# Attention operands spread anew over GpSimd, VectorE and ScalarE, and a pair's weighted sums in one stretch

## The chip, the cores and the metric

The kernel runs on one core of one Trainium2 chip. The metric is device time in microseconds for one execution, the median of several runs. The kernel before takes 841.28 us (three runs, 840.67 to 841.33). The engines that matter are TensorE (PE: matrix products and transposes into PSUM), VectorE (DVE), ScalarE (ACT), GpSimd (POOL) and the queue of SyncE (SP), which issues most transfers.

## The reference

Attention over 4 batches, 8 heads, 576 positions and 64 columns per head, with a causal mask in blocks of 64; then a mixture of eight experts (one per token) and a last two-layer network. The change touches the attention alone:

```python
scores = scale * np.matmul(q, k.transpose(0, 1, 3, 2))
scores = np.where(mask, scores, -1000000000.0)
scores = scores - np.max(scores, axis=-1, keepdims=True)
attn = np.exp(scores)
attn = attn / (np.sum(attn, axis=-1, keepdims=True) + 1e-09)
return np.matmul(attn, v).astype(np.float32)
```

## The kernel before, in words

Attention goes over 16 pairs of heads (`n` = 0 to 15). A pair has seven steps (`z` = 0 to 6), one block of scores each: 64-position blocks are taken two by two, for one head or for both. In most pairs the order of the blocks is `ORDER` = 3, 1, 0, 4, 2, 6, 5. Block 6 (`kinds` 4, all 576 columns, both heads) comes at step 5.

In each step TensorE makes the scores of the step (`scores`, tile `s`) and then transposes the exponentials of the block two steps earlier (`flip`, tile `pt`). VectorE takes the row maxima (`nmax`, lines 339, 344, 348), ScalarE the exponentials (line 350, tile `pall`), and one of them copies `pt` into `pT` (line 379 on ScalarE, line 511 on VectorE).

A score is a product in three terms: each of `q` and `k` is split into a high part of reduced precision and the low part that is left. `qa` holds the high and low parts of q, `qb` copies of the high parts, `kd` k's high parts twice (in both halves of the partitions), `kl` k's low parts, `qf` and `kT` the plain values for block 0. `load_q` and `load_k` make these for the pair after the one whose scores are running.

What stands between the steps is in a table, `PLAN`: the key is (step, place), where place 0 is ahead of the step's scores, 1 behind the scores, and 2 behind the step's softmax. "q" and "k" transpose the next pair's operands into PSUM (`psq`, `psk`) and split them. A tuple such as (0, 3) makes the weighted sums of the pair before over those blocks of keys (`weigh`, tile `px`, line 393, in halves of TensorE's columns). "first" makes the sums of the first 64 positions (`py`, line 408), and, where the pair is the second of two, puts the row factors in place on VectorE (`row_order`, lines 429 and 435). "store" copies `px` to `xT` and, where the pair is the second of two, puts four or five rows on a list. "rows" takes one of that list (tile `xr`, line 445, then two VectorE operations, lines 451 and 455, and a store).

PSUM has eight banks. Two hold `s`, two `pt` and `py`, two `px` and `xr` (tag "x"), and the last two are one buffer of tag "big". That one buffer is taken in turn by `psq`, `psk` and the scores of block 6: the next owner's first matmul waits until every reader of the owner before is done.

Each engine works its instructions off in the order of the program. Behind the attention, the routing and the experts follow; the first steps of the routing are laid between the steps of pairs 14 and 15. Rows that are still on the list when attention ends are made at the start of the experts (`begin`).

Of the kernel before, what the change touches and what calls it, by code (L numbers as in the profile page):

```python
# [11 lines left out]
F32 = mybir.dt.float32  # L12
# [6 lines left out]
ALU = mybir.AluOpType  # L19
# [6 lines left out]
P = 128  # L26
B, H, S, D = 4, 8, 576, 64
# [5 lines left out]
E, F = 8, 1024  # L33
# [16 lines left out]


ORDER_FIRST, ORDER_LAST, ORDER = (2, 4, 0, 1, 5, 6, 3), (3, 1, 4, 2, 6, 0, 5), (3, 1, 0, 4, 2, 6, 5)
PLAN = {(1, 0): ["rows", "q"], (2, 0): ["sum"], (2, 2): ["k", (0, 3)], (3, 0): ["rows"],
        (4, 2): [(3, 5)], (5, 0): ["first"], (5, 1): ["store"], (6, 2): ["rows"]}
FROM = 0, 128, 256, 320, 448
LAG = 2
COPY = 4
ON_ACT = (0, 2, 3, 4, 5)


KDUP = (1, 1, 0, 0), (0, 0, 1, 1)
SMALL = (1, 1, 1, 1, 1, 1, 1, 2), (2, 2, 2, 2, 1, 1, 2, 2)
EARLY = 3, 2
WARM = 30, 2
BIG = 3e38
# [57 lines left out]
def attention(late, weights, tc, q, k, v, ids, w_gate, mbias, x_dram, dram, ident, tabs):  # L123
# [3 lines left out]
    nc = tc.nc  # L127
# [6 lines left out]
    wk = ctx.enter_context(tc.tile_pool(name="a_wk", bufs=2))  # L134
# [47 lines left out]
    def turned(dst, x):  # L182
        if x.dtype == F32R:
            nc.tensor.transpose(dst.bitcast(F32R), x, identr)
        else:
            nc.tensor.transpose(dst, x, ident)
# [20 lines left out]
    qzs = [one.tile([P, P], F32R, name=f"qz{i}") for i in range(2)]  # L207
# [34 lines left out]

    qk = {}

    def eng(n, x):
        return nc.gpsimd if SMALL[n > 0][x] == 2 else nc.vector

    def load_q(n):
        psq = ps2.tile([P, 1024], F32, tag="big", name=f"psq{n}")
        psq = psq[:, 64:64 + S]  # L250
        for t, x in enumerate(FROM):
            turned(psq[:, x:x + P], io_t[n, "q"][:, t, :])
        qa, qb, qf = qas[n % 2], qbs[n % 2], qfs[n % 2]

        qT = wk.tile([P, 9, 64], F32, tag="qT", name=f"qT{n}", bufs=1)
        nc.scalar.activation(qT, psq.rearrange("p (i t) -> p i t", t=64), AF.Copy, scale=D ** -0.5)
        for h in range(2):
            hs, oh = slice(h * 64, h * 64 + 64), slice(64 - h * 64, 128 - h * 64)
            nc.scalar.copy(qa[hs, h, :7], qT[hs, 2:])
            eng(n, h).tensor_tensor(qa[oh, h, :7], qT[hs, 2:], qa[hs, h, :7].bitcast(F32), op=ALU.subtract)  # L260
        for h in range(2):
            hs = slice(h * 64, h * 64 + 64)
            (nc.gpsimd.tensor_copy if n else nc.scalar.copy)(
                qf[hs, h].rearrange("p (i t) -> p i t", t=64), qT[hs, :2])
        eng(n, 4).tensor_copy(qb[:64, :7], qa[:64, 0, :7])
        eng(n, 5).tensor_copy(qb[64:, 7], qa[64:, 1, 6])
        eng(n, 6).tensor_copy(qb[64:, 8:], qa[64:, 1, :6])
        eng(n, 7).tensor_copy(qzs[n % 2][:, 64:], qa[:, 1, 6])

    def load_k(n):  # L270
        if n:
            psk = ps2.tile([P, 1024], F32, tag="big", name=f"psk{n}")[:, 64:64 + S]
            ranges = [(psk, slice(0, S))]
        else:

            pk = [ps2.tile([P, 512], F32, tag="x", name=f"psk{n}_{i}", bufs=2) for i in range(2)]
            ranges = [(pk[0][:, :448], slice(0, 448)), (pk[1][:, :P], slice(448, S))]
        for t, x in enumerate(FROM):
            if n:
                dst = psk[:, x:x + P]  # L280
            else:
                dst = pk[t // 4][:, x % 448:x % 448 + P]
            turned(dst, io_t[n, "k"][:, t, :])
        kT = wk.tile([P, S], F32, tag="kT", name=f"kT{n}")
        for a, cs in ranges:
            nc.vector.tensor_copy(kT[:, cs], a)
        kd = wk.tile([P, 2, S], F32R, tag="kd", name=f"kd{n}")
        kl = wk.tile([P, S], F32R, tag="kl", name=f"kl{n}")
        for h in range(2):
            hs, oh = slice(h * 64, h * 64 + 64), slice(64 - h * 64, 128 - h * 64)  # L290
            for u, dst in enumerate((kd[hs, h], kd[oh, h])):
                e = KDUP[n > 0][2 * h + u]
                if e == 0:
                    for a, cs in ranges:
                        nc.scalar.copy(dst[:, cs], a[hs])
                else:
                    (nc.vector if e == 1 else nc.gpsimd).tensor_copy(dst, kT[hs])
            eng(n, 2 + h).tensor_tensor(kl[hs], kT[hs], kd[hs, h].bitcast(F32), op=ALU.subtract)
        qk[n] = kT, kd, kl

    pTs, nmaxs = {}, {}
# [84 lines left out]
    def weigh(n, k0, k1):  # L386

        if k0 == 0:
            pxs[n] = ps2.tile([P, 512], F32, tag="x", name=f"px{n}", bufs=2)
        for kk in range(k0, k1):  # L390
            s0 = max(64, kk * P)
            for h in range(2):
                nc.tensor.matmul(pxs[n][h * 64:(h + 1) * 64, s0 - 64:], io_t[n, "v"][:, kk, h * D:(h + 1) * D],  # L393
                                 pTs[n][:, kk, h, s0:], start=(kk == 0), stop=(kk == 4))

    def store_xT(n):
        b, c = divmod(n, NP)
        nc.scalar.copy(xT[:, c, b % 2 * S + 64:(b % 2 + 1) * S], pxs.pop(n))

    def weigh_first(n, order=True):  # L400

        b, c = divmod(n, NP)
        if n < B * NP - 1:
            px = ps1.tile([P, 512], F32, tag="pt", name=f"py{n}", bufs=4 - SB)
        else:
            px = ps2.tile([P, 512], F32, tag="x", name=f"py{n}", bufs=2)
        for h in range(2):
            nc.tensor.matmul(px[h * 64:(h + 1) * 64, :64], io_t[n, "v"][:, 0, h * D:(h + 1) * D],
                             pTs[n][:, 0, h, :64], start=True, stop=True)
        if c % 2 and order:  # L410
            row_order(b, c // 2)
        nc.scalar.copy(xT[:, c, b % 2 * S:b % 2 * S + 64], px[:, :64])

    def row_sums(b, a):

        r = rinv[:, b, 2 * a:2 * a + 2]
        nc.vector.tensor_scalar(r, ssum[:, b, 2 * a:2 * a + 2], 1e-9, None, op0=ALU.add)
        nc.vector.reciprocal(r, r)
# [18 lines left out]
    def rows(j, a, spare=False, xr=None):  # L437

        if spare:
            px = ps2.tile([P, 1024], F32, tag="big", name=f"xr{j}_{a}")  # L440
        else:
            px = ps2.tile([P, 512], F32, tag="x", name=f"xr{j}_{a}", bufs=2)
        w = P + 2 * E
        for c in range(2):
            nc.tensor.matmul(px[:, c * w:(c + 1) * w], xT[:, 2 * a + c, j % NB * P:(j % NB + 1) * P],
                             rh[:, 2 * a + c, :], start=True, stop=True)
        if xr is None:
            xr = keep.tile([P, 256], F32, tag="xr", name=f"xrow{j}_{a}", bufs=4)
        pv = px[:, :2 * w].rearrange("p (c w) -> p c w", w=w)
        rv = rt[:, j, 4 * a:4 * a + 4].rearrange("p (c h) -> p c h", h=2)  # L450
        nc.vector.tensor_tensor(
            xr.rearrange("p (c h d) -> p c h d", c=2, h=2),
            pv[:, :, :P].rearrange("p c (h d) -> p c h d", h=2),
            rv.unsqueeze(3).to_broadcast([P, 2, 2, D]), op=ALU.mult)
        nc.vector.tensor_tensor(
            lg[:, j, 4 * a:4 * a + 4, :].rearrange("p (c h) e -> p c h e", h=2),
            pv[:, :, P:].rearrange("p c (h e) -> p c h e", h=2),
            rv.unsqueeze(3).to_broadcast([P, 2, 2, E]), op=ALU.mult)
        nc.sync.dma_start(out=x_dram[j * P:(j + 1) * P, a * 256:(a + 1) * 256], in_=xr)
# [9 lines left out]
    def act(n, z, at):  # L469

        if n >= B * NP:
            return
        for what in PLAN.get((z, at), ()):
            if what == "q" and n + 1 < B * NP:
                load_q(n + 1)
            elif what == "k" and n + 1 < B * NP:
                load_k(n + 1)
            elif what == "rows" and todo:
                done.add(todo[0])
                rows(*todo.pop(0))  # L480
            elif n == 0:
                continue
            elif isinstance(what, tuple):
                weigh(n - 1, *what)
            elif what == "sum" and (n - 1) % 2:
                row_sums((n - 1) // NP, (n - 1) % NP // 2)
            elif what == "first":
                weigh_first(n - 1)
            elif what == "store":
                store_xT(n - 1)  # L490
                if (n - 1) % 2:
                    todo.extend((j, (n - 1) % NP // 2) for j in rows_of[(n - 1) // NP])
# [5 lines left out]
    for g in range(len(steps) + LAG):  # L498
        n, z = divmod(g, NK)
# [1081 lines left out]
```

## Time and profile before

| | |
|---|---|
| median of three runs | 841.28 us |
| the profiled execution | 839.69 us |
| its span | 837.8 us |
| PE busy | 817.9 us (98%) |
| DVE busy | 608.3 us (73%) |
| ACT busy | 495.6 us (59%) |
| POOL busy | 205.4 us (25%) |

The attention is the first 224 us or so of the span. The rows below name instructions by the lines of the kernel before. In a timeline neighbouring instructions of one group stand in one row, whose duration runs from the first one's start to the last one's end. Matmuls overlap, so the step from one row's start to the next is the better measure of what TensorE spends.

### The profile page before, as it was taken

What the parts mean: (1) busy time and instruction counts of PE and PEld (TensorE: products, weight loads), DVE (VectorE), ACT (ScalarE), POOL (GpSimd) and SP (SyncE); (2) the same over time, 40 slices, a digit from 0 to 9 for tenths busy, and PEclk for the clock granted to TensorE, in tenths of its full rate; (3) what the DMA queues carried; (4) which work ended last, traced back from release to release, by engine and by line L of the source; (5) the groups of instructions that cost most, each with busy time, mean ns of one, the idle gap of its engine ahead of it and who ended that gap; (6) DMA issues with size and microseconds to landing.
All of it is one profiled execution on the core that took longest, in us unless ns stands there. A gap on an engine that the chain in (4) does not pass through costs nothing. (4 is left out here: it accounts for less than half of the span.)

```text
span 837.8 us, 13997 instructions
## 1 busy us (share of the span) xinstructions
PE 817.9 (98%) x4936; PEld 709.3 (85%) x4936; DVE 608.3 (73%) x1115; ACT 495.6 (59%) x994; POOL 205.4 (25%) x249
## 2 busy tenths in 40 slices
PE   6999999998899999999999999999999999999998
PEld 5777777775788888888888999999999988888887
DVE  6788888789666656797873766766636877777774
ACT  5898888896533334464544666766657644444442
POOL 8546556546301212120202000110000011112120
PEclk6999999999999999999999999999999999999999
DMA  6445655630744447765625453453644633333301
GB/s 155 119 125 144 172 145 134 171 95 20 247 131 150 153 125 234 240 204 163 203 84 162 142 176 121 170 175 134 218 120 160 239 143 128 125 126 126 132 32 38
DMA packets 138058, 123.17 MB, mean 147 GB/s; under 512 B 70183, under 2 KB 122423, under 8 KB 135296
## 3 DMA queue, kind: packets, MB, share of 16 engines
q1 hardware_dynamic: 132256, 107.98, 41.9%
q0 software_dynamic: 4384, 13.92, 4.7%
q8 instruction: 40, 0.66, 0.3%
q10 hardware_dynamic: 1344, 0.33, 0.2%
q14 instruction: 34, 0.28, 0.1%
HBM read 89.17 MB, written 40.37 MB: 155 GB/s over the span
## 5 line engine op out<-in xcount | busy, mean ns | idle before, releaser
L1019 PE MATMUL h<-yhi,wi 128*128 128x384 f32 x768 | 200.4, 338 | 1.1 <-ACTq L1253 1.1
L1019 PEld LDWEIGHTS h<-yhi,wi 128*128 128x128 f32 x768 | 139.5, 188 | 1.5 <-ACTq L1253 1.5
L1019 PE MATMUL h<-ylo,wi 128*128 128x384 f32 x384 | 129.2, 337 | 0.0
L1293 ACT ACTIVATE cl<-h,half 128x384 f32<-128x384 f32 x96 | 55.9, 582 | 69.4 <-PE h L1019 69.1
L350 ACT ACTIVATE pall<-s,nmax 128x384 f32<-128x384 f32 (+2 forms) x144 | 79.5, 558 | 28.1 <-DVE nmax L344 17.0
L1297 DVE SCALAR_TENSOR_TENSOR gg<-cl,h 128x384 f32<-128x384 f32 x96 | 52.3, 552 | 51.8 <-ACT cl L1294 49.7
L1423 PE MATMUL p<-wo,s 128*128 128x256 f32 (+1 forms) x432 | 87.8, 338 | 0.0
L1423 PEld LDWEIGHTS p<-wo,s 128*128 128x128 f32 x432 | 68.5, 188 | 9.2
L1478 POOL DMA_INDIRECT out_dram<-rest,tab x16 | 27.3, 1707 | 190.9 <-DVE rest L1445 185.4
L1019 PEld LDWEIGHTS h<-ylo,wi 128*128 128x128 f32 x384 | 72.1, 188 | 0.0
L368 PE MATMUL pt<-ident,pall 128*128 128x128 f32 x400 | 65.7, 282 | 5.5 <-DVE pT L511 3.5
L1423 PE MATMUL p<-wo,a 128*128 128x256 f32 (+1 forms) x330 | 66.0, 335 | 0.0
L1019 PE MATMUL h<-xhi,wh 128*128 128x512 f32 (+2 forms) x164 | 63.1, 385 | 0.0
L1019 PE MATMUL h<-xhi,wl 128*128 128x512 f32 (+2 forms) x164 | 61.7, 376 | 0.5 <-DVE wl L1103 0.5
L1019 PE MATMUL h<-xlo,wh 128*128 128x512 f32 (+2 forms) x164 | 61.6, 376 | 0.0
L1128 PE MATMUL acc<-wh,hl 128*128 128x512 f32 x152 | 59.6, 392 | 0.1
L1423 PEld LDWEIGHTS p<-wo,a 128*128 128x128 f32 x330 | 52.8, 188 | 7.9
L1128 PE MATMUL acc<-wl,hh 128*128 128x512 f32 x152 | 59.3, 390 | 0.0
L1128 PE MATMUL acc<-wh,hh 128*128 128x512 f32 x152 | 59.1, 389 | 0.0
L393 PE MATMUL px<-pT,v 128*64 128x448 f32 (+4 forms) x320 | 54.5, 432 | 0.0
L1294 ACT ACTIVATE cl<-cl 128x384 f32<-128x384 f32 x96 | 50.5, 526 | 3.0
L368 PEld LDWEIGHTS pt<-ident,pall 128*128 128x128 f32 x400 | 43.9, 143 | 7.0 <-issue 3.1
(316 smaller groups left out, 1807.8 us busy)
## 6 DMA issues: line engine op xcount, KB each, us to landing
raw<-in_moe_w_dram SPq DMA_DIRECT2D x80, 256.0 KB
g_dram<-gg SPq DMA_DIRECT2D x48, 384.0 KB
g<-g_dram SPq DMA_DIRECT2D x18, 1024.0 KB
wi_raw<-in_moe_w_in_dram SPq DMA_DIRECT2D x16, 512.0 KB
wo_raw<-in_moe_w_out_dram SPq DMA_DIRECT2D x16, 512.0 KB
yr<-y_dram SPq DMA_DIRECT2D x18, 256.0 KB
x_dram<-xrow SPq DMA_DIRECT2D x33, 128.0 KB
v<-in_v_dram SPq DMA_DIRECT2D x32, 128.0 KB
```

What stands on the lines that cost most here:

```text
L350: nc.scalar.activation(pall[n % 2][:, o:o + w], pss[:, u:u + w], AF.Exp, bias=nm[:, x:x + 1], scale=1.0, accum_out=ssum[:, b, c, x:x + 1])
L368: nc.tensor.transpose(pt[:, kk, :], pa[:, o + kk * P:o + (kk + 1) * P], ident)
L393: nc.tensor.matmul(pxs[n][h * 64:(h + 1) * 64, s0 - 64:], io_t[n, "v"][:, kk, h * D:(h + 1) * D], pTs[n][:, kk, h, s0:], start=(kk == 0), ...
L1019: nc.tensor.matmul(ps, a[za], b[zb], start=(i == 0), stop=(i == n - 1))
L1128: nc.tensor.matmul(accs[s][u], a[:, us], b[:, 1, :], start=(f == 0 and i == 0), stop=(f == NF - 1 and i == 2))
L1293: nc.scalar.activation(cl, ph, AF.Relu, bias=half, scale=0.5)
L1294: nc.scalar.activation(cl, cl, AF.Square)
L1297: nc.vector.scalar_tensor_tensor(gg[:, :, f % 2, :], cl.rearrange(t3, t=P), 1.0, ph.rearrange(t3, t=P), op0=ALU.min, op1=ALU.max)
L1423: nc.tensor.matmul(o, a, b, start=(x == 0 and i in FRESH), stop=(x == len(terms) - 1), skip_group_check=True)
L1478: outs.append(nc.gpsimd.indirect_dma_start(out=out[:, :], out_offset=bass.IndirectOffsetOnAxis(ap=tabs.tab[:, j, 0:1].bitcast(U32), axis=0 ...
```

## The change

Four things change. The high parts of q go from ScalarE to GpSimd, for every pair but the first, with all that `load_q` copies besides. k's high parts are wanted twice per head; ScalarE made both of the first head from PSUM and VectorE both of the second from `kT`. Now ScalarE makes one per head from PSUM, and GpSimd makes the other from it. The low parts of k are subtracted on VectorE straight from PSUM, at a place "low" of their own in the table; only 128 columns of plain k are still copied. And the weighted sums of all five blocks with "first" stand in one stretch behind step 2, with "store" in step 3 and the rows at step 4 where step 3 had them.

```diff
--- before.py
+++ after.py
@@ -50,16 +50,15 @@
 ORDER_FIRST, ORDER_LAST, ORDER = (2, 4, 0, 1, 5, 6, 3), (3, 1, 4, 2, 6, 0, 5), (3, 1, 0, 4, 2, 6, 5)
-PLAN = {(1, 0): ["rows", "q"], (2, 0): ["sum"], (2, 2): ["k", (0, 3)], (3, 0): ["rows"],
-        (4, 2): [(3, 5)], (5, 0): ["first"], (5, 1): ["store"], (6, 2): ["rows"]}
+PLAN = {(1, 0): ["rows", "q"], (2, 0): ["sum"], (2, 2): ["k", (0, 5), "first"], (3, 1): ["store"],
+        (3, 2): ["low"], (4, 0): ["rows"], (6, 2): ["rows"]}
 FROM = 0, 128, 256, 320, 448
 LAG = 2
 COPY = 4
 ON_ACT = (0, 2, 3, 4, 5)
-KDUP = (1, 1, 0, 0), (0, 0, 1, 1)
-SMALL = (1, 1, 1, 1, 1, 1, 1, 2), (2, 2, 2, 2, 1, 1, 2, 2)
+KDUP = 1, 1, 0, 0
 EARLY = 3, 2
 WARM = 30, 2
 BIG = 3e38
@@ -242,9 +241,6 @@
     qk = {}
-    def eng(n, x):
-        return nc.gpsimd if SMALL[n > 0][x] == 2 else nc.vector
-
     def load_q(n):
         psq = ps2.tile([P, 1024], F32, tag="big", name=f"psq{n}")
         psq = psq[:, 64:64 + S]
@@ -254,18 +250,24 @@
         qT = wk.tile([P, 9, 64], F32, tag="qT", name=f"qT{n}", bufs=1)
         nc.scalar.activation(qT, psq.rearrange("p (i t) -> p i t", t=64), AF.Copy, scale=D ** -0.5)
-        for h in range(2):
-            hs, oh = slice(h * 64, h * 64 + 64), slice(64 - h * 64, 128 - h * 64)
-            nc.scalar.copy(qa[hs, h, :7], qT[hs, 2:])
-            eng(n, h).tensor_tensor(qa[oh, h, :7], qT[hs, 2:], qa[hs, h, :7].bitcast(F32), op=ALU.subtract)
-        for h in range(2):
-            hs = slice(h * 64, h * 64 + 64)
-            (nc.gpsimd.tensor_copy if n else nc.scalar.copy)(
-                qf[hs, h].rearrange("p (i t) -> p i t", t=64), qT[hs, :2])
-        eng(n, 4).tensor_copy(qb[:64, :7], qa[:64, 0, :7])
-        eng(n, 5).tensor_copy(qb[64:, 7], qa[64:, 1, 6])
-        eng(n, 6).tensor_copy(qb[64:, 8:], qa[64:, 1, :6])
-        eng(n, 7).tensor_copy(qzs[n % 2][:, 64:], qa[:, 1, 6])
+        E = nc.gpsimd if n else nc.vector
+        copy = nc.gpsimd.tensor_copy if n else nc.scalar.copy
+        halves = [(h, slice(h * 64, h * 64 + 64), slice(64 - h * 64, 128 - h * 64)) for h in range(2)]
+        for h, hs, oh in halves:
+            copy(qa[hs, h, :7], qT[hs, 2:])
+            if not n:
+                E.tensor_tensor(qa[oh, h, :7], qT[hs, 2:], qa[hs, h, :7].bitcast(F32), op=ALU.subtract)
+        if n:
+            for h, hs, oh in halves:
+                E.tensor_tensor(qa[oh, h, :7], qT[hs, 2:], qa[hs, h, :7].bitcast(F32), op=ALU.subtract)
+        for h, hs, oh in halves:
+            copy(qf[hs, h].rearrange("p (i t) -> p i t", t=64), qT[hs, :2])
+        E.tensor_copy(qb[:64, :7], qa[:64, 0, :7])
+        E.tensor_copy(qb[64:, 7], qa[64:, 1, 6])
+        E.tensor_copy(qb[64:, 8:], qa[64:, 1, :6])
+        nc.gpsimd.tensor_copy(qzs[n % 2][:, 64:], qa[:, 1, 6])
+
+    low_k = {}
     def load_k(n):
         if n:
@@ -281,21 +283,28 @@
             else:
                 dst = pk[t // 4][:, x % 448:x % 448 + P]
             turned(dst, io_t[n, "k"][:, t, :])
-        kT = wk.tile([P, S], F32, tag="kT", name=f"kT{n}")
-        for a, cs in ranges:
-            nc.vector.tensor_copy(kT[:, cs], a)
+        kT = wk.tile([P, S if n == 0 else P], F32, tag="kT" if n else "kT0", name=f"kT{n}", bufs=2 if n else 1)
         kd = wk.tile([P, 2, S], F32R, tag="kd", name=f"kd{n}")
         kl = wk.tile([P, S], F32R, tag="kl", name=f"kl{n}")
-        for h in range(2):
-            hs, oh = slice(h * 64, h * 64 + 64), slice(64 - h * 64, 128 - h * 64)
-            for u, dst in enumerate((kd[hs, h], kd[oh, h])):
-                e = KDUP[n > 0][2 * h + u]
-                if e == 0:
-                    for a, cs in ranges:
-                        nc.scalar.copy(dst[:, cs], a[hs])
-                else:
-                    (nc.vector if e == 1 else nc.gpsimd).tensor_copy(dst, kT[hs])
-            eng(n, 2 + h).tensor_tensor(kl[hs], kT[hs], kd[hs, h].bitcast(F32), op=ALU.subtract)
+        halves = [(h, slice(h * 64, h * 64 + 64), slice(64 - h * 64, 128 - h * 64)) for h in range(2)]
+        if n:
+            nc.vector.tensor_copy(kT, psk[:, :P])
+            for h, hs, oh in halves:
+                nc.scalar.copy(kd[hs, h], psk[hs])
+            for h, hs, oh in halves:
+                nc.gpsimd.tensor_copy(kd[oh, h], kd[hs, h])
+            low_k[n] = [(kl[hs], psk[hs], kd[hs, h].bitcast(F32)) for h, hs, oh in halves]
+        else:
+            for a, cs in ranges:
+                nc.vector.tensor_copy(kT[:, cs], a)
+            for h, hs, oh in halves:
+                for u, dst in enumerate((kd[hs, h], kd[oh, h])):
+                    if KDUP[2 * h + u] == 0:
+                        for a, cs in ranges:
+                            nc.scalar.copy(dst[:, cs], a[hs])
+                    else:
+                        nc.vector.tensor_copy(dst, kT[hs])
+                nc.vector.tensor_tensor(kl[hs], kT[hs], kd[hs, h].bitcast(F32), op=ALU.subtract)
         qk[n] = kT, kd, kl
     pTs, nmaxs = {}, {}
@@ -475,6 +484,9 @@
                 load_q(n + 1)
             elif what == "k" and n + 1 < B * NP:
                 load_k(n + 1)
+            elif what == "low" and n + 1 in low_k:
+                for dst, a, b in low_k.pop(n + 1):
+                    nc.vector.tensor_tensor(dst, a, b, op=ALU.subtract)
             elif what == "rows" and todo:
                 done.add(todo[0])
                 rows(*todo.pop(0))
```

TensorE, steps 2 to 5 of pair 7 before (`px6`, `py6` are pair 6's weighted sums, `s7_6` block 6 of pair 7):

```order
L393 MATMUL px6_1578<-pT6_1374,v6_918 64x320 x2
L445 MATMUL xr6_0_1589<-rh_161,xT_162 128x144 x2
L326 MATMUL s7_4_1596<-kd7_1391,qa1_137 128x512
...
L326 MATMUL s7_2_1608<-kd7_1391,qa1_137 128x384
...
L368 MATMUL pt7_0_0_1612<-ident_65,pall1_158 128x128 x2
L393 MATMUL px6_1578<-pT6_1374,v6_918 64x192 x2
L393 MATMUL px6_1578<-pT6_1374,v6_918 64x64 x2
L408 MATMUL py6_1622<-pT6_1374,v6_918 64x64 x2
L316 MATMUL s7_6_1626<-kd7_1391,qa1_137 128x288
```

The same stretch in the changed kernel:

```order
L402 MATMUL px6_1583<-pT6_1374,v6_918 64x320 x2
L402 MATMUL px6_1583<-pT6_1374,v6_918 64x192 x2
L402 MATMUL px6_1583<-pT6_1374,v6_918 64x64 x2
L417 MATMUL py6_1594<-pT6_1374,v6_918 64x64 x2
L335 MATMUL s7_4_1602<-kd7_1390,qa1_137 128x512
...
L454 MATMUL xr7_0_1617<-rh_161,xT_162 128x144 x2
L335 MATMUL s7_2_1624<-kd7_1390,qa1_137 128x384
...
L377 MATMUL pt7_0_0_1628<-ident_65,pall1_158 128x128 x2
L325 MATMUL s7_6_1634<-kd7_1390,qa1_137 128x288
```

The sums of the last two blocks and `py` stood between the transposes of step 4 and block 6; they now stand ahead of step 3. One row (`xr`) stands between step 3 and block 6, before in step 3's front and now behind its transposes.

VectorE from step 1 to step 5 of pair 7 before (`qb0`, `kT8`, `kd8` belong to pair 8):

```order
L265 COPY qb0_138<-qa0_136 64x448
L266 COPY qb0_138<-qa0_136 64x64
L344 TENSOR_REDUCE nmax7_1488<-s7_1_1534 128x2
L344 TENSOR_REDUCE nmax7_1488<-s7_0_1549 128x2
L286 COPY kT8_1568<-psk8_1562 128x576
L297 CAST kd8_1570<-kT8_1568 64x576 x2
...
L348 TENSOR_REDUCE nmax7_1488<-s7_4_1596 128x1
L511 COPY pT7_1553<-pt7_1_0_1600 128x2x2x128
L348 TENSOR_REDUCE nmax7_1488<-s7_2_1608 128x1
L339 TENSOR_REDUCE nmax7_1488<-s7_6_1626 128x1
```

And in the changed kernel:

```order
L353 TENSOR_REDUCE nmax7_1495<-s7_1_1541 128x2
L353 TENSOR_REDUCE nmax7_1495<-s7_0_1556 128x2
L291 COPY kT8_1575<-psk8_1569 128x128
L357 TENSOR_REDUCE nmax7_1495<-s7_4_1602 128x1
L523 COPY pT7_1560<-pt7_1_0_1607 128x2x2x128
L489 TENSOR_TENSOR kl8_1577<-psk8_1569,kd8_1576 64x576 x2
...
L357 TENSOR_REDUCE nmax7_1495<-s7_2_1624 128x1
L348 TENSOR_REDUCE nmax7_1495<-s7_6_1634 128x1
```

The casts of `qb`, most of `kT` and the doubles `kd` are gone; two subtractions that read `psk8` stand behind the copy of step 3.

GpSimd's work for pair 8 before (`qa0`, `qb0`, `qz0` and `kl8` belong to it):

```order
L263 COPY qf0_140<-qT8_1522 64x128 x2
L260 TENSOR_TENSOR qa0_136<-qT8_1522,qa0_136 64x448 x2
L267 COPY qb0_138<-qa0_136 64x384
L268 COPY qz0_142<-qa0_136 128x64
L298 TENSOR_TENSOR kl8_1571<-kT8_1568,kd8_1570 64x576 x2
```

And in the changed kernel:

```order
L257 CAST qa0_136<-qT8_1529 64x448 x2
L262 TENSOR_TENSOR qa0_136<-qT8_1529,qa0_136 64x448 x2
L264 COPY qf0_140<-qT8_1529 64x128 x2
L265 COPY qb0_138<-qa0_136 64x448
L266 COPY qb0_138<-qa0_136 64x64
L267 COPY qb0_138<-qa0_136 64x384
L268 COPY qz0_142<-qa0_136 128x64
L295 COPY kd8_1576<-kd8_1576 64x576 x2
```

The two subtractions for `kl` went; the casts of `qa`, two copies into `qb` and two copies of `kd` came.

## Rows read from the trace of the kernel before

**Rows 1.** Windows: length, busy us (instructions) per engine, PE clock, DMA share, GB/s.

```profile
12.15:24.69 12.54, 11.81 (x62) 9.72 (x62) 8.13 (x14) 9.35 (x26) 7.59 (x10) 0.63 0.72 176
36.34:186.46 150.12, 149.25 (x1152) 113.52 (x1150) 123.26 (x265) 130.90 (x361) 83.66 (x100) 1.00 0.55 143
```

**Rows 2.** TensorE's timeline, one pair: start, duration, operation, count, idle before.

```profile
101.78 2.76 PE L393 MATMUL px<-pT,v 128*64 128x512 f32 x12
104.47 0.76 PE L445 MATMUL xr<-rh,xT 128*128 128x144 f32 x4
104.97 0.49 PE L326 MATMUL s<-kd,qa 128*128 128x512 f32 x1
105.53 0.20 PE L329 MATMUL s<-maskk,maskq 128*128 128x64 bf16 x1
...
106.78 0.66 PE L393 MATMUL px<-pT,v 128*64 128x192 f32 x8
107.49 0.40 PE L316 MATMUL s<-kd,qa 128*128 128x288 f32 x1
...
109.69 0.66 PE L445 MATMUL xr<-rh,xT 128*128 128x144 f32 x4
110.09 0.43 PE L326 MATMUL s<-kd,qa 128*128 128x384 f32 x1
```

**Rows 3.** VectorE's timeline beside it.

```profile
101.55 0.85 DVE L266 CAST qb<-qa 64x64 fp32r<-64x64 f32 x1 [0.20 <-ACT qa L259]
102.42 1.02 DVE L344 TENSOR_REDUCE nmax<-s 128x2 f32<-128x512 f32 x2
...
105.77 0.69 DVE L348 TENSOR_REDUCE nmax<-s 128x1 f32<-128x512 f32 x1
106.38 0.68 DVE L511 COPY pT<-pt 128x512 f32<-128x512 f32 x1
106.98 0.55 DVE L348 TENSOR_REDUCE nmax<-s 128x1 f32<-128x384 f32 x1
```

**Rows 4.** ScalarE's timeline there.

```profile
100.36 1.15 ACT L259 CAST qa<-qT 64x448 fp32r<-64x448 f32 x2
101.54 0.59 ACT L379 COPY pT<-pt 128x512 f32<-128x512 f32 x1
```

**Rows 5.** Groups of instructions by line: busy us, mean ns, idle before.

```profile
L298 DVE TENSOR_TENSOR kl<-kT,kd 64x576 fp32r<-64x576 f32 x2 | 1.5, 754 | 0.1
L77 DVE TENSOR_TENSOR xlo<-xt,xhi 128x512 fp32r<-128x512 f32 x8 | 5.4, 690 | 8.2 <-ACT xhi L76 8.0 <-issue 0.2
...
L298 POOL TENSOR_TENSOR kl<-kT,kd 64x576 fp32r<-64x576 f32 x30 | 45.2, 1505 | 11.6 <-DVE kd L297 9.8
L267 POOL CAST qb<-qa 64x384 fp32r<-64x384 f32 x15 | 7.6, 506 | 0.9
```

**Rows 6.** TensorE's timeline in the last pair.

```profile
205.67 2.37 PE L393 MATMUL px<-pT,v 128*64 128x512 f32 x12
207.97 0.51 PE L445 MATMUL xr<-rh,xT 128*128 128x144 f32 x2
```

**Rows 7.** TensorE's timeline in an even pair.

```profile
63.87 2.95 PE L393 MATMUL px<-pT,v 128*64 128x512 f32 x12
66.75 0.50 PE L326 MATMUL s<-kd,qa 128*128 128x512 f32 x1
...
68.57 0.66 PE L393 MATMUL px<-pT,v 128*64 128x192 f32 x8
69.59 0.40 PE L316 MATMUL s<-kd,qa 128*128 128x288 f32 x1
```

**Rows 8.** VectorE's timeline under the routing of the first slots.

```profile
190.27 1.12 DVE L265 CAST qb<-qa 64x448 fp32r<-64x448 f32 x1
...
194.95 0.94 DVE L297 CAST kd<-kT 64x576 fp32r<-64x576 f32 x2
```

**Rows 9.** VectorE's timeline in the even pair of group 7.

```profile
69.77 1.12 DVE L429 COPY rt<-rinv 128x16 f32<-128x16 f32 x1
```

## The prediction

> **What bounds the kernel now.** I read the engines' shares by stretch first. In the twelve pairs from 36.34 to 186.46 us TensorE is busy 149.25 of 150.12 us at the full granted clock (1.00, the 2.4 GHz level), ScalarE 130.90, VectorE 123.26, GpSimd 83.66 [rows 1]. A pair takes 150.12 / 12 = 12.51 us, and TensorE hardly ever has nothing in flight. So whatever moves the attention must move TensorE: by shortening what it runs, or by making it wait. Since matmuls overlap, I then took TensorE's timeline of one pair and read the steps from start to start, not the durations [rows 2]. The other engines' timelines beside it [rows 3, 4] tell what each was doing while TensorE was in the weighted sums.
>
> Two things are to be seen there. VectorE stands behind ScalarE's casts of q: the cast of 64 columns runs from 101.55 for 0.85 us, and the maxima of step 1 begin only at 102.42 [rows 3]. ScalarE spends 1.15 us on those casts ahead of the copy of `pT` at 101.54 for which the weighted sums wait [rows 4]. And between the start of step 3's mask product (105.53) and block 6 (107.49) TensorE has 1.96 us of work [rows 2]; that is the cover under which the one "big" buffer of PSUM has to come free, since block 6 takes it from `psk`.
>
> **The change, part by part.**
>
> *The low parts of k on VectorE, from PSUM.* This is the part that decides. Before, the last readers of `psk` were ScalarE's copies and the copy of `kT`. Now the two subtractions read it too, and they stand on VectorE behind step 3's maxima and behind its copy into `pT`. How late that is can be read off: the mask product starts at 105.53, the maxima at 105.77, the copy at 106.38, VectorE is free at 106.98, thus 1.45 us behind the mask [rows 2, 3]. Nothing of this chain can come earlier, since each link needs step 3's scores or transposes. For one subtraction of 64x576 with one operand in PSUM there is no row. Below it lies the 128x512 one with an operand in PSUM, 690 ns, above it the same shape out of SBUF on VectorE in the first pair, 754 ns [rows 5]; as shape and count of columns agree I take 754. Two are 1.51 us, so the buffer is free 1.45 + 1.51 = 2.96 us behind the mask, and with 0.04 us of handing over (the maxima start 0.04 us after the mask's end, 105.73) block 6 starts 3.00 us behind it.
>
> When would TensorE be there? Of the 1.96 us, 0.71 (106.78 to 107.49) were the second stretch of weighted sums, which is gone from this place: 1.25 is left. A row of `xr` comes in, 0.40 us (109.69 to 110.09) [rows 2]. Less 0.05 to 0.1 for entering the sums that no longer follow, it is there after about 1.6 us. It waits 3.00 - 1.60 = 1.40 us, in every pair, with all of its later work behind it; VectorE's maxima of step 4 are then late too, but their exponentials are wanted only two steps on, and by the durations above they arrive about when TensorE does. With 690 ns the wait is 1.27; were the subtraction to cost 0.9, it is 1.7.
>
> *The weighted sums in one stretch.* The first stretch takes 2.69 us from its start to the next row's in pair 7 [rows 2], but 2.30 in the last pair, where nothing was waited for [rows 6]. In an even pair, where step 3 follows directly, it takes 2.88, and the second stretch takes 1.02 (68.57 to 69.59) against the 0.71 of pair 7 [rows 7]. A row of `xr` behind the sums takes 0.50 (104.47 to 104.97) and elsewhere 0.40, so leaving the stretch costs about 0.1, and I take the same for entering. So, odd pairs gain 0.39 of waits and 0.2 for one entry and exit less, 0.59; even pairs 2.88 - 2.40 = 0.48 (2.30 and 0.1 for leaving, which the row behind it carries there), 0.31 of the second stretch and 0.2, 0.99. Mean 0.79. The waits go because ScalarE no longer has its 1.15 us of casts there and VectorE no longer stands behind them.
>
> In the Trainium skill, "TensorEngine Tiling (Array Packing)", section Key Properties, a change of tiling mode drains TensorE. The 0.50 against 0.40 agrees with that in kind; the page has no price. Without such a drain the gain would be 0.2 less per pair.
>
> *q and the doubles of k on GpSimd.* GpSimd loses two subtractions of 1505 ns and gains two casts of 448 columns, two small copies and two copies of 576. A one-operand cast of 384 columns takes 506 ns [rows 5]; by columns 0.6 and 0.75 us. So 3.0 us go and about 1.2 + 0.8 + 1.5 = 3.5 come, on an engine busy 83.66 of 150.12. At worst (each copy at the 1505 of two operands) it is 3 us more, and the doubles are wanted only at step 0 of the next pair, over 4 us after block 6's old place. I cost it at nothing.
>
> *What VectorE and ScalarE are rid of* costs nothing where TensorE sets the pace. It counts in pair 14, where the routing's first steps fill VectorE: there `qb` (1.12 and some 0.4), the doubles (0.94) [rows 8] and 0.45 of `kT` go, 1.5 comes and one row's 0.6 of VectorE moves in: about -0.8 us. The rows' list is one step earlier in each pair, so one of six rows left over for the experts' start is already made: -0.4 us.
>
> *Sum.* Per pair +1.40 - 0.79 = +0.61 us, for the 13 pairs 1 to 13: +7.9. Pair 0 has no weighted sums and runs at a mean clock of 0.63 [rows 1], so TensorE is slower to arrive and waits little: +0.3. With -0.8 and -0.4 this is +7.0 us. On the profiled execution's 839.69 (its span 837.8 and 1.9 around it) that is 846.7; the median of the runs shown is 1.6 higher, 841.28, and from there it is 848.3. I say 848.3, for the pairs' terms with their bounds 844 to 854.
>
> **The rivals.**
>
> *More hidden waits in TensorE's steps.* A busy TensorE is modelled, and 0.39 us of waits were found within one group that shows no idle time. If each of the other steps holds some hundredths, VectorE and ScalarE freed would give back up to 0.5 us more per pair. Then it is +0.11 x 13 + 0.3 - 1.2 = +0.5, so 842. Against it: the same transposes and scores take equal steps in pairs of different load.
>
> *The wait is covered.* If the subtractions are over when TensorE arrives (a later TensorE, a VectorE that is ahead by what it no longer does), only the gains are left: -0.79 x 13 - 1.2 = -11.5, so 830. For it speaks that VectorE comes to step 3 with nothing left over. Against it speaks that the 1.45 us are counted from step 3's own scores, and that TensorE has lost just the 0.71 us that stood before block 6. It decides as soon as the wait is under 0.8 us a pair.
>
> *GpSimd holds VectorE up ahead of step 3.* In the even pairs VectorE puts the row factors in place; one such copy took 1.12 us [rows 9], where a copy of so few columns should take a fraction: it ran while GpSimd was at its subtractions. These three or four copies now stand right ahead of step 3's maxima, with GpSimd at work all along. If each waits out one instruction of up to 1.2 us, VectorE comes 0.7 to 2 us late to step 3, and block 6 with it: 1.3 x 7 even pairs = +9 more, 857. Against it: VectorE is otherwise idle for some 3 us there.
>
> The Trainium skill has a rule for this, "SBUF — State Buffer", section Who interferes with whom: the port pair that VectorE and GpSimd share is locked for a whole instruction, and the loser is blocked. The 1.12 us agrees with it; by that rule each of the copies may lose an instruction's length, and this rival is the result.
>
> **How the numbers follow.** The forecast has 0.62, the hidden waits 0.13, the covered wait 0.17, GpSimd's hold 0.08. About 0.2% (1.7 us) is what a measurement of this kernel tells from no change, so same is 839.6 to 843.0: the hidden waits' 842, less a point for its upper half, 0.12. Faster is the covered wait, 0.17. Slower is the rest, 0.71. The range has to take in 842 and part of the covered wait (a wait half gone is 836) and GpSimd's hold up to its middle: 834 to 856. The forecast's own range is 844 to 854.
>
> **What would show it.** In the profile after, block 6's first product stands behind an idle stretch of 1.2 to 1.5 us, released by VectorE's subtraction of `kl`; the weighted sums with `py` take about 3.0 us in one piece; a pair takes 13.1 us against 12.51, and the subtraction 0.75 us. The cast of `qb` is gone from in front of step 1's maxima. Wrong would be: no idle time at block 6 (the covered wait), a wait released by GpSimd at step 0, row factors of over a microsecond ahead of step 3, or a subtraction far from 0.75 us.

## The result and the profile after

The changed kernel takes 845.4 us (median of 6 runs, 844.2 to 846.5) against 841.3 of the kernel before on the same chip: the ratio is 1.0053, with 95% interval 1.0042 to 1.0065. Its profiled execution took 846.50 us, of which the span is 844.7; that of the kernel before was 839.69 with a span of 837.8. The two profiled executions thus lie 6.8 us apart, the medians 4.1.

Nearly all names of the code stay; the lines have moved by nine or so. Step 3's scores are L335 and L336, its mask product L338, the transposes L377, the weighted sums L402 and L417, block 6 is L325, a row of `xr` L454, the subtractions for `kl` L489. First come the windows of the changed kernel (columns as in [rows 1]): pair 1, and then the twelve pairs 2 to 13.

```profile
24.18:38.29 14.11, 12.41 (x89) 9.43 (x88) 7.86 (x17) 9.70 (x29) 6.75 (x12) 0.88 0.54 130
38.29:196.57 158.28, 142.44 (x1152) 110.11 (x1150) 116.02 (x242) 116.69 (x337) 82.68 (x148) 1.00 0.50 132
```

Twelve pairs take 158.28 us, 13.19 each, against the 12.51 worked out from [rows 1]. TensorE's busy time has fallen (142.44 us), and so have VectorE's and ScalarE's; the twelve pairs are longer because TensorE is idle for 15.8 us of them, before for 0.9. What TensorE waits for is told by its waits in that stretch (us in total, times, longest):

```profile
PE s L325 <- DVE kl L489: 15.1, 12, 1.3
PE pt L377 <- ACT pall L359: 0.7, 4, 0.2
```

There is one wait that counts, in each of the twelve pairs (1.2 us in odd ones, 1.3 in even ones), and it has the subtractions of `kl` as its releaser. No wait is put down to GpSimd. TensorE's timeline in an odd pair, the places that answer to [rows 2]:

```profile
107.30 2.81 PE L402 MATMUL px<-pT,v 128*64 128x512 f32 x20
109.94 0.29 PE L417 MATMUL py<-pT,v 128*64 128x64 f32 x4
110.16 0.50 PE L335 MATMUL s<-kd,qa 128*128 128x512 f32 x1
...
110.73 0.20 PE L338 MATMUL s<-maskk,maskq 128*128 128x64 bf16 x1
...
113.75 0.40 PE L325 MATMUL s<-kd,qa 128*128 128x288 f32 x1 [1.20 <-DVE kl L489]
```

The weighted sums are one piece from 107.30 to 110.16, 2.86 us. From step 3's mask product (110.73) to block 6 (113.75) it is 3.02 us; in the even pairs it is 3.12. VectorE beside it, as in [rows 3]:

```profile
105.75 0.69 DVE L353 TENSOR_REDUCE nmax<-s 128x2 f32<-128x512 f32 x1 [0.23 <-PE s L338]
...
107.41 0.29 DVE L291 COPY kT<-psk 128x128 f32<-128x128 f32 x1 [0.28 <-PE psk L183]
110.97 0.69 DVE L357 TENSOR_REDUCE nmax<-s 128x1 f32<-128x512 f32 x1 [3.27 <-PE s L338]
111.58 0.68 DVE L523 COPY pT<-pt 128x512 f32<-128x512 f32 x1
112.17 1.51 DVE L489 TENSOR_TENSOR kl<-psk,kd 64x576 fp32r<-64x576 f32 x2
```

Step 1's maxima (105.75) come with no cast of `qb` ahead of them. Then VectorE idles for 3.27 us until step 3's scores are there, reduces, copies `pT`, and only then starts the subtractions, which end at 113.68; block 6 starts 0.07 later. The groups of the attention (columns as in [rows 5]):

```profile
L489 DVE TENSOR_TENSOR kl<-psk,kd 64x576 fp32r<-64x576 f32 x30 | 22.6, 753 | 0.9 <-ACT kd L293 0.6
L295 POOL CAST kd<-kd 64x576 fp32r<-64x576 f32 x30 | 19.9, 663 | 2.1 <-ACT kd L293 0.3
L257 POOL CAST qa<-qT 64x448 fp32r<-64x448 f32 x30 | 16.7, 556 | 79.7 <-ACT qT L252 78.8
...
L325 PE MATMUL s<-kd,qa 128*128 128x288 f32 x32 | 11.3, 354 | 19.3 <-DVE kl L489 19.3
```

One subtraction took 753 ns; GpSimd's casts of `qa` 556 and its doubles of k 663. All of block 6's idle time, 19.3 us, is put down to `kl`.

### The profile page after: what moved, and what is told of

Its sections match the earlier page's. It is cut to its first block, busy times and chain, and to the rows that moved or that the text cites. A ratio compares the mean times of both kernels' runs of the same rounds, so it can differ in the third digit from the quotient of the medians.

```text
span 844.7 us, 14003 instructions
## 1 busy us (share of the span) xinstructions
PE 809.8 (96%) x4936; PEld 705.0 (83%) x4936; DVE 597.8 (71%) x1085; ACT 478.3 (57%) x964; POOL 203.2 (24%) x309
## 5 line engine op out<-in xcount | busy, mean ns | idle before, releaser
L377 PE MATMUL pt<-ident,pall 128*128 128x128 f32 x400 | 65.4, 282 | 1.7 <-DVE pT L523 0.9
L357 DVE TENSOR_REDUCE nmax<-s 128x1 f32<-128x384 f32 (+1 forms) x64 | 39.6, 620 | 37.3 <-PE s L338 37.0
L1112 ACT CAST wh<-raw 128x1024 fp32r<-128x1024 f32 x40 | 41.9, 1050 | 13.1 <-PE acc L1140 13.0
```

Of the source, the lines that this page charges most:

```text
L357: nc.vector.tensor_reduce(nm[:, x:x + 1], pss, axis=AX.X, op=ALU.max, negate=True)
L377: nc.tensor.transpose(pt[:, kk, :], pa[:, o + kk * P:o + (kk + 1) * P], ident)
L1112: nc.scalar.copy(ws[s, f][0], weights.raw[s, f])
```

## The experiments

What the theory says: the change loses because the two subtractions, as the last readers of the buffer "big", stand behind step 3's maxima and copy, so that block 6 gets the buffer some 1.4 us late. The rivals: the new operand work itself is dear (more instructions on GpSimd, which also holds VectorE up), or the one stretch of sums harms.

**The subtractions sooner.** They are put at once behind the copies of k, ahead of step 3's maxima:

```diff
-(2, 2): ["k", (0, 5), "first"], ... (3, 2): ["low"],
+(2, 2): ["k", "low", (0, 5), "first"],
```

> The changed kernel, with k's low parts subtracted right behind the 128 columns of plain k in step 2 instead of behind step 3's work. Theory (the one big PSUM buffer is freed too late): VectorE has some 3 us of nothing to do while TensorE is in the weighted sums, ScalarE's copies of k end before those sums do, so both subtractions are over before step 3's maxima; the wait of 1.2 to 1.3 us at block 6 goes in all 15 pairs that have it, a pair takes about 11.95 us against 13.19, and the time is about 827 us (824 to 832). Rival (the buffer's late release only hides other lateness, of ScalarE's copies or of GpSimd's doubles): VectorE now stands behind ScalarE's copies ahead of step 3, the maxima of step 3 come late, and no more than half of the wait is won: 836 us or more.

Measured: 840.0 us, 0.9996 (0.9984 to 1.0007). The wait at block 6 was gone, but the time missed its forecast by 13 us. Odd pairs took 11.9 us, as expected, even ones 12.8 to 15.9. VectorE in an even pair, whose step 3's mask product started at 118.25:

```profile
117.50 1.52 DVE L489 TENSOR_TENSOR kl<-psk,kd 64x576 fp32r<-64x576 f32 x2 [2.28 <-ACT kd L293]
119.05 0.43 DVE L438 COPY rt<-rinv 64x16 f32<-64x16 f32 x2
119.52 0.72 DVE L444 COPY rt<-rinv 64x2 f32<-64x2 f32 x2
120.27 0.69 DVE L357 TENSOR_REDUCE nmax<-s 128x1 f32<-128x512 f32 x1
```

`kl` comes only at 117.50, since it waits for both of ScalarE's copies (idle 2.28), and the row factors of the even pair (L438, L444) stand behind it in the program. So step 3's maxima start at 120.27, and TensorE stands still at step 4:

```profile
121.83 0.66 PE L377 MATMUL pt<-ident,pall 128*128 128x128 f32 x4 [0.97 <-ACT pall L359]
...
123.33 0.50 PE L335 MATMUL s<-kd,qa 128*128 128x512 f32 x1 [0.69 <-ACT pall L359]
...
124.40 1.17 PE L454 MATMUL xr<-rh,xT 128*128 128x144 f32 x4
```

Behind the waits of 0.97 and 0.69 us the products are slow: four of `xr` take 0.79 us from 124.40 to the next row (125.19), where they took 0.40 before. The windows of this pair and of the one behind it show the granted clock:

```profile
111.95:127.80 15.85, 14.19 (x103) 11.16 (x102) 10.75 (x26) 10.71 (x32) 8.33 (x16) 0.89 0.51 137
127.80:139.70 11.90, 11.58 (x98) 9.08 (x97) 7.97 (x19) 8.62 (x25) 6.77 (x12) 1.00 0.54 141
```

At 0.89 the pair was in part at the lower of the two levels. The theory of the wait stands, but something in the order behind the subtractions was left out: the row factors.

**The subtractions last.** The same, with the row factors ahead of them:

```diff
-(2, 2): ["k", "low", (0, 5), "first"],
+(2, 2): ["k", (0, 5), "first", "low"],
```

> As e1_low_early, but the subtractions stand behind the row factors of step 2 instead of ahead of them. In e1's odd pairs the wait was gone and a pair took 11.9 us; in its even pairs VectorE did the row factors between the subtractions and step 3's maxima, and a pair took 12.8 to 15.9. Theory (the row factors fit into the 2.3 us in which VectorE waits for ScalarE's copies): even pairs take about 12.3 us (one more row than the odd ones), odd pairs 11.9 as in e1, time about 831 us (828 to 835). Rival (GpSimd is at work all along, so the row factors take their 2 us, hold the subtractions up and the even pairs stay as they were): 838 us or more.

Measured: 834.1 us, 0.9929 (0.9912 to 0.9946). Only the order of VectorE's work at one place differs from the run above, and 0.7% of the time went with it. Twelve pairs took 146.88 us, 12.24 each; odd ones 11.87. The waits of TensorE in them:

```profile
PE pt L377 <- ACT pall L359: 4.3, 14, 0.3
```

**The copies of k a half step sooner too.** Those 0.3 us at the transposes are left because the subtractions still wait for ScalarE's copies and push the maxima back. So `load_k` moves to behind step 2's scores, ahead of that step's transposes and exponentials:

```diff
-(2, 2): ["k", (0, 5), "first"], ... (3, 2): ["low"],
+(2, 1): ["k"], (2, 2): [(0, 5), "first", "low"],
```

> As e5_low_last, with the next pair's k transposed ahead of step 2's exponentials instead of behind them, so that ScalarE's copies of k come about 1.2 us earlier. Theory: the subtractions are over before step 3's maxima are wanted, and the 0.3 us that the transposes of step 6 still wait for exponentials go too: 0.2 to 0.4 us a pair less than e5, about 827 us (823 to 831). Rival: step 2's exponentials are now late by as much, and the time is that of e5 or more.

Measured: 827.6 us (4 runs, 827.2 to 828.2), 0.9851 (0.9831 to 0.9871). It beats both kernels (it is called the best version below), and the same instructions run in it as in the changed kernel: 13.19 us per pair became 142.57 / 12 = 11.88, by places alone. Its window, and VectorE in an even pair:

```profile
34.95:177.52 142.57, 140.70 (x1151) 109.55 (x1150) 115.64 (x241) 117.15 (x337) 82.72 (x148) 1.00 0.58 149
```

```profile
61.64 0.80 DVE L438 COPY rt<-rinv 128x16 f32<-128x16 f32 x1
62.35 1.27 DVE L444 COPY rt<-rinv 64x2 f32<-64x2 f32 x2
63.63 1.52 DVE L489 TENSOR_TENSOR kl<-psk,kd 64x576 fp32r<-64x576 f32 x2
65.19 0.69 DVE L357 TENSOR_REDUCE nmax<-s 128x1 f32<-128x512 f32 x1
```

The row factors take 2 us and the subtractions 1.52. The subtractions fill the time in which VectorE is idle there in the changed kernel; they end at 65.15, and the maxima of step 3 start at 65.19, 0.42 us behind the mask product, where it was 0.24. TensorE goes from the mask product (64.77) to block 6 without a stop:

```profile
64.77 0.21 PE L338 MATMUL s<-maskk,maskq 128*128 128x64 bf16 x1
...
66.16 0.41 PE L377 MATMUL pt<-ident,pall 128*128 128x128 f32 x2
66.33 0.38 PE L325 MATMUL s<-kd,qa 128*128 128x288 f32 x1
```

That is 1.56 us; in the changed kernel 3.02.

**The suspected work twice.** Each subtraction is issued two times:

```diff
-for dst, a, b in low_k.pop(n + 1):
+for dst, a, b in 2 * low_k.pop(n + 1):
```

> The changed kernel with both subtractions of k's low parts done twice over, same result. Theory (each microsecond of VectorE between step 3 and the buffer's release is a microsecond of TensorE): the wait at block 6 grows from 1.25 to 2.76 us, time about 867 us (863 to 870). Rival (TensorE would have waited elsewhere anyway and the pair has slack behind block 6): under half of that, below 857 us.

Measured: 884.4 us, 1.0545 (1.0507 to 1.0583). The wait grew as forecast, to 2.8 to 2.9 us, but pairs 2 to 13 took 15.8 us on average, and the whole 17 us more than the forecast from the wait alone. Block 6's products behind one wait tell why, and the windows of this pair and the next:

```profile
85.09 0.61 PE L325 MATMUL s<-kd,qa 128*128 128x288 f32 x1 [2.92 <-DVE kl L489]
...
85.73 0.44 PE L325 MATMUL s<-kl,qb 128*128 128x288 f32 x1
85.97 0.44 PE L325 MATMUL s<-kd,qa 128*128 128x288 f32 x1
```

```profile
74.12:91.89 17.77, 14.85 (x102) 11.82 (x101) 12.43 (x26) 10.25 (x29) 6.78 (x12) 0.81 0.28 77
91.89:106.20 14.31, 11.35 (x94) 8.62 (x93) 9.63 (x19) 9.14 (x27) 6.78 (x12) 1.00 0.57 149
```

Block 6's products stand 0.24 us apart (85.73 to 85.97), in the changed kernel 0.13: TensorE went on at the lower level after the long wait. Of pairs 2 to 13, five were granted 1.00 and took 1.6 us more than the same pair of the changed kernel, by which the way from the mask product to block 6 had grown; the other seven, at 0.81 to 0.90, took 2.9 to 4.2 us more. There a wait cost more than its own length; at 1.2 to 1.3 us, in the changed kernel's twelve pairs, the clock stayed at 1.00.

**The operands alone.** The changed kernel's operand work with before's places for the sums, and the subtractions behind step 3's copy as in the changed kernel; the table is shown against before's:

```diff
-(2, 2): ["k", (0, 3)], (3, 0): ["rows"],
+(2, 2): ["k", (0, 3)], (3, 0): ["rows"], (3, 2): ["low"],
```

> The changed kernel's operands with the kernel before's places for the sums, the store and the rows; k's low parts stay behind step 3's work. Theory: the buffer is again free 3.0 us behind step 3's mask product, and TensorE is there after 1.96 us, so it waits 1.0 us in each pair; the sums' first stretch loses its 0.4 to 0.5 us of waits; +0.55 us a pair, time about 847 us (844 to 851). Rival (the freed ScalarE and VectorE are worth more than the 0.4 us): 841 us or less with the wait still there.

Measured: 844.6 us, 1.0043 (1.0026 to 1.0059). The waits, from pair 2 to pair 13:

```profile
PE s L325 <- DVE kl L489: 11.9, 12, 1.0
```

The second stretch of sums stands ahead of block 6 again and covers 0.3 us more of the wait than the row did. A pair takes 155.72 / 12 = 12.98 us. So the operands with their place make the loss.

**The sums alone.** Before's operands, with the changed kernel's places:

```diff
-(2, 2): ["k", (0, 3)], (3, 0): ["rows"], (4, 2): [(3, 5)], (5, 0): ["first"], (5, 1): ["store"],
+(2, 2): ["k", (0, 5), "first"], (3, 1): ["store"], (4, 0): ["rows"],
```

> The kernel before with only the weighted sums of a pair in one stretch behind step 2, the store in step 3 and the rows at step 4; the operands are made as before. Theory (one stretch saves one entry and one exit, the second stretch's waits in even pairs go, and nothing waits for PSUM, since ScalarE's copies of k end early enough): a gain of 0.3 to 0.5 us a pair, time about 836 us (833 to 839), no idle time at block 6. Rival (the loss of the changed kernel comes from moving the sums, which takes away the work that stood ahead of block 6): a wait at block 6 here too, 842 us or more.

Measured: 853.1 us, 1.0144 (1.0125 to 1.0164), a miss of 17 us on the other side. There is no wait at block 6. Odd pairs took 11.7 to 11.8 us, even ones 15.0 to 15.4, and one 17.6 at a granted clock of 0.90. VectorE in such a pair, then GpSimd beside it:

```profile
70.08 1.30 DVE L429 COPY rt<-rinv 128x16 f32<-128x16 f32 x1
71.28 1.56 DVE L435 COPY rt<-rinv 64x2 f32<-64x2 f32 x2
72.76 0.68 DVE L348 TENSOR_REDUCE nmax<-s 128x1 f32<-128x512 f32 x1
```

```profile
69.72 3.09 POOL L298 TENSOR_TENSOR kl<-kT,kd 64x576 fp32r<-64x576 f32 x2 [1.04 <-DVE kd L297]
```

The factors of a few columns took 1.30 and 1.56 us while GpSimd was at its subtractions (69.72 to 72.81). Step 3's mask product started at 69.86, its maxima only at 72.76; TensorE waited 0.91 us at step 4's transposes, and 0.66 before that at the row (`xr`), for ScalarE's copy of `xT`. This is the rival of GpSimd's hold on VectorE, in a kernel in which VectorE had no idle time to hide it.

**The sums alone, with the row factors late.** The "order" of the even pairs goes behind step 4; the diff is against the run above:

```diff
-(2, 2): ["k", (0, 5), "first"], (3, 1): ["store"], (4, 0): ["rows"],
+(2, 2): ["k", (0, 5), "first"], (3, 0): ["rows"], (3, 1): ["store"], (5, 0): ["order"],
...
-                weigh_first(n - 1)
+                weigh_first(n - 1, False)
+            elif what == "order":
...
```

> The kernel before with the weighted sums in one stretch, as e2_sums_only, but with the row factors left at step 5 and the rows at step 3, where they were. e2 lost its time in even pairs alone (15 us against 11.7 in odd ones), where two row-factor rows took 1.30 and 1.56 us of VectorE ahead of step 3's maxima while GpSimd was at its subtractions. Theory (GpSimd's hold on VectorE, the fourth case of the prediction, was e2's loss, not the stretch): even pairs come to about 12.1 us, time about 836 us (832 to 840). Rival (the one stretch itself starves ScalarE with the operands of before): 846 us or more.

Measured: 837.0 us, 0.9957 (0.9942 to 0.9971). So the loss of the run above goes with the factors' early place (one row moved by a step along with them, which was not separated). In the windows:

```profile
36.13:184.29 148.16, 146.71 (x1151) 118.26 (x1150) 123.35 (x265) 129.34 (x361) 83.74 (x100) 1.00 0.55 143
```

148.16 / 12 = 12.35 us per pair: in before's operands the one stretch is worth 0.16.

**q as before.** The changed kernel with the old `load_q`: the casts of `qa` on ScalarE, `qb` on VectorE.

```diff
-            copy(qa[hs, h, :7], qT[hs, 2:])
+            nc.scalar.copy(qa[hs, h, :7], qT[hs, 2:])
...
-        E.tensor_copy(qb[:64, :7], qa[:64, 0, :7])
+        eng(n, 4).tensor_copy(qb[:64, :7], qa[:64, 0, :7])
```

> The changed kernel with q's parts made as before (the casts on ScalarE, two copies on VectorE). Theory (freeing ScalarE of 1.15 us of casts is what took the waits out of the weighted sums): the stretch of sums grows from 2.86 to about 3.2 us, the wait at block 6 stays 1.2 us, +0.4 us a pair, about 850 us (848 to 855). Rival (only the doubles of k and their earlier copies mattered): the sums stay at 2.9 us and the time at 845 to 846.

Measured: 855.6 us, 1.0176 (1.0155 to 1.0198), just over the forecast's upper end; a pair 164.25 / 12 = 13.69, 0.50 more than in the changed kernel. The sums in an odd pair, and block 6 behind them:

```profile
84.49 2.93 PE L403 MATMUL px<-pT,v 128*64 128x512 f32 x17
...
87.74 0.50 PE L336 MATMUL s<-kd,qa 128*128 128x512 f32 x1
...
91.44 0.40 PE L326 MATMUL s<-kd,qa 128*128 128x288 f32 x1 [1.32 <-DVE kl L490]
```

The stretch takes 3.25 us (84.49 to 87.74) against 2.86, with a wait within it that no row shows as idle. From the mask product to block 6 it is 0.1 more than in the changed kernel. In even pairs 0.67 us of the idle time stood at a row instead, which waited for ScalarE's copy of `xT`; they too took 0.5 us longer. So ScalarE and VectorE rid of q's casts are worth 0.4 in the stretch and 0.5 in the pair; which of the two engines gives how much was not separated.

**The sums apart again.** The best version with before's places for the sums:

```diff
-(2, 1): ["k"], (2, 2): [(0, 5), "first", "low"], (3, 1): ["store"], (4, 0): ["rows"],
+(2, 1): ["k"], (2, 2): [(0, 3), "low"], (3, 0): ["rows"], (4, 2): [(3, 5)], (5, 0): ["first"], (5, 1): ["store"],
```

> As e6_k_sooner, with the weighted sums in two stretches and the store and the rows at the places of the kernel before. With no wait left at block 6 or in the sums, this prices the one stretch by itself. Theory (one entry into TensorE's half-column mode and one exit cost 0.1 us each, and the second stretch's small sums wait for VectorE in even pairs): 0.2 to 0.35 us a pair more than e6, about 831 us (829 to 834). Rival (with the operands ready, two stretches cost no more than one): 828 us or less.

Measured: 833.3 us, 0.9922 (0.9908 to 0.9935), 0.7% of the whole more than the best version, and inside the forecast. The window of its pairs, however, is nearly that of the best version, so the forecast's 0.2 to 0.35 us a pair did not come:

```profile
34.62:177.72 143.10, 142.96 (x1151) 108.11 (x1150) 109.79 (x241) 117.73 (x337) 82.92 (x148) 1.00 0.58 150
```

143.10 / 12 = 11.93 us against 11.88. The sums of an odd pair in it:

```profile
96.82 2.37 PE L402 MATMUL px<-pT,v 128*64 128x512 f32 x12
99.12 0.76 PE L454 MATMUL xr<-rh,xT 128*128 128x144 f32 x4
99.62 0.48 PE L335 MATMUL s<-kd,qa 128*128 128x512 f32 x1
...
101.44 0.66 PE L402 MATMUL px<-pT,v 128*64 128x192 f32 x8
...
102.14 0.40 PE L325 MATMUL s<-kd,qa 128*128 128x288 f32 x1
```

The stretches take 2.30 (96.82 to 99.12) and 0.70 us (101.44 to 102.14), and the row behind the first 0.50, where a row elsewhere takes 0.40. In the whole window TensorE is idle for 0.14 us, and for 142.57 - 140.70 = 1.87 us in the best version: what the one stretch saves in TensorE's own work, it gives back for the most part in short waits for exponentials. In the two profiled executions 2.8 of the spans' 3.0 us (828.4 and 825.4) lie behind pair 14's first products, where the routing fills VectorE. Most of it, 2.4 us, lies ahead of the experts' first product: from pair 14's first to it the sums apart take 31.80 us, the best version 29.42. What makes it there, the places of the sums or those of the store and the rows, was not separated. The medians lie 5.7 us apart; both profiled executions were the fastest of their runs, and no profile shows the other 2.7.

## Why the prediction came out

*The wait at block 6* was right link by link. A subtraction took 753 ns for 754, the buffer came free 3.02 us behind the mask product for 3.00 (3.12 in even pairs), and TensorE would have been there after 1.56 us for 1.6 (the distance in the best version, where nothing is waited for). By starts the wait is 3.02 - 1.56 = 1.46 us in odd pairs and 1.56 in even ones, 1.51 on average, forecast 1.40; the trace shows 1.2 to 1.3 of it as idle. The runs show that it is this wait: taken away by places alone, it gave 11.88 us per pair; with the subtractions issued twice, block 6 came 1.6 us later still.

*The weighted sums in one stretch* came out in their size, and by the reasons given. The pair grew by 0.68, so the gains were 1.51 - 0.68 = 0.83, forecast 0.79. The step put 0.2 of it to one entry and exit less: in the best version with the sums apart, the two stretches and the 0.10 in the row make 3.10, in one piece it is 2.86. That is 0.24. In the best version itself its waits of 0.14 per pair leave little of that. The rest the step put down to ScalarE and VectorE, which no longer make q's operands: 0.5 by the run with q as before. So the term is named after the sums, but most of it is the operands'; with before's operands the one stretch alone gained 0.16. The Trainium skill's rule on a change of tiling mode ("TensorEngine Tiling (Array Packing)", Key Properties), that it drains TensorE, agrees with the 0.24 us in kind.

*GpSimd for nothing* was right: its busy time in twelve pairs is 82.68 us against 83.66 [rows 1], and no wait of TensorE ends on it. The estimates of 0.6 and 0.75 us for its copies stand against 0.56 and 0.66.

*The ends* were both under-sized, and nearly cancel. The step said that pair 0 waits little (+0.3) and pair 1 as the others; from the span's start to pair 2 it was +1.95 us (36.34 to 38.29), for 0.9. Block 6 waited 1.76 and 1.70 us there, and pair 1 ran at a granted clock of 0.88, in 14.11 us, where before it took 11.65 at 1.00. Before, the slow spell lay in pair 0, at 0.63 [rows 1]. So the clock fell one pair later, and the loss is not the wait's alone. At the other end, from pair 14's first products to the experts' first, it was 2.7 us shorter (32.54 before, 29.82 after), where -0.8 was forecast for what VectorE is rid of. With the operands alone the same stretch took 31.51 us, so 1.0 goes with them, near the forecast; the other 1.7 came only with the new places of sums, store and rows, which the step had at nothing there. The row less at the experts' start, forecast -0.4, was there, but TensorE then waited 0.45 us for VectorE; from the experts' first product to the first of 512 columns it was 0.2 less (10.87 to 10.70).

*The sum* was +7.0 us, and the two profiled executions differ by 6.8. That is closer than its terms: pairs 2 to 13 came to 8.2 for 7.3, the start to 1 more and the end to 1.7 less than forecast, so the agreement is in part luck. Set on the median of before it came to 848.3, which is 2.9 over the median of after: before's profiled execution lay 1.6 below its median and after's 1.1 above. The step of adding one execution's difference to a median is what was off; what makes executions of one kernel differ by these few us stays open.

*The rivals.* The hidden waits were to give up to 0.5 us a pair more; the gains of 0.83, for 0.79 without them, leave room for 0.04. The covered wait did not come, but its mechanism was real: with another place for the subtractions it is the best version, at 827.6 for the 830 that this rival gave. GpSimd's hold on VectorE was there in the changed kernel too. VectorE in an even pair of it:

```profile
67.88 0.84 DVE L438 COPY rt<-rinv 128x16 f32<-128x16 f32 x1
68.62 1.27 DVE L444 COPY rt<-rinv 64x2 f32<-64x2 f32 x2
71.23 0.69 DVE L357 TENSOR_REDUCE nmax<-s 128x1 f32<-128x512 f32 x1 [1.34 <-PE s L338]
```

The factors took 2.0 us from 67.88 to 69.89, but 1.34 us of idle time were left behind them until step 3's scores: it cost nothing, because VectorE had nothing else there. The prediction had named such row factors ahead of step 3 as a sign that it is wrong; the sign came, and the forecast held. In the two runs where VectorE or GpSimd had `kl` at this place, even pairs took up to 3.7 us more than odd ones at the full granted clock (15.4 against 11.7 in the sums alone), and up to 6 where the clock fell too. The Trainium skill's rule ("SBUF — State Buffer", Who interferes with whom), that the engine which comes first holds the shared port pair for its whole instruction while the other is blocked, fits the three copies of few columns in the sums alone, which took from 70.08 to 72.84 beside subtractions that end at 72.81; it tells nothing of what they hold up, which decided. The prediction named what speaks against this rival here, VectorE's idle 3 us; the expectations of those two runs, which filled or moved that idle time, did not take it up, and both missed.

## What to carry to other kernels

Work that is moved to an engine with idle time has to be put where its inputs come in and ahead of that engine's next due work; the idle time stands at one place of the loop, not everywhere. The last reader of a shared PSUM buffer in program order can set when its next owner starts, as it did here, so count from that reader's start, link by link, against the time at which TensorE would come. And before moving the work that stood ahead of a wait, count it as cover: here the second stretch of sums had covered 0.3 us of it.

## What the runs showed of the hardware

TensorE's granted clock fell in some windows with long waits: in the run with the subtractions twice, with one wait of 2.8 to 2.9 us in each pair, it was 0.81 to 0.90 in 7 of the 12 pairs 2 to 13 and 1.00 in the other 5; it was 0.89 in a pair with waits of 0.97 and 0.69 (the subtractions sooner), 0.90 in one with 1.73 and 0.69 (the sums alone), and 1.00 in the changed kernel's twelve pairs with waits of 1.2 to 1.3. Against the best version the single wait cost 2.0% (1.0053 / 0.9851), the doubled one 7.0% (1.0545 / 0.9851). Two copies of two columns by 64 rows on VectorE (L444; L435 with before's operands) took 0.33 us together in the kernel before, as GpSimd's subtractions ended, 0.72 beside GpSimd's doubles of k (the subtractions sooner), 1.27 beside its work on q (the changed kernel), and 1.56 beside its subtractions for `kl` (the sums alone).
